# One V projection per quad, one PSUM bank for the output sums, 37 resident weight halves

## The chip, the cores and the metric

The kernel runs on one core of a Trainium2 chip. That core has five engines with queues of their own: TensorE (PE; its weight loads are shown apart, as PEld) multiplies, VectorE (DVE) and ScalarE (ACT) work on tiles in SBUF and read the PSUM accumulators, GpSimd (POOL) works on SBUF alone, and SyncE (SP) issues DMAs. The metric is the device time of one execution in microseconds (us): the median of the runs.

## The reference

An input of 2048 rows by 640 features goes through four layers, each added to its input after a layer norm: A, B, A, B.

Layer A is attention with a recurrent memory. The rows are cut into 64 segments of 32. To each segment the 8 rows of memory are put in front, so that 40 rows are worked on:

```python
for s in range(n_seg):
    h = jnp.concatenate([mem, xs], axis=1)
    q, k, v = (einsum('btd,dhe->bhte', h, W) for W in (Wq, Wk, Wv))
    p = softmax(mask(q @ k.T * scale))
    o = einsum('bhte,hed->btd', p @ v, Wo)
    mem = o[:, :M, :].copy()
    outs.append(o[:, M:, :])
```

There are 32 heads of 192. The memory of a segment is the first 8 rows of the output of the one before, so the segments follow one another.

Layer B is attention with 32 heads of 20 in which a row sees eight rows: itself and those 2, 4 and so on to 14 rows before it.

## The kernel before

**Lanes and steps.** The two A layers run side by side as two lanes. Lane 1 (the second A layer) is two segments (LAG = 2) behind lane 0. A step `t` works on segment t in lane 0 and segment t - 2 in lane 1; both use the same weights, so one matmul has 80 columns, 40 of each lane. There are 66 steps with layer A and one last step with B alone. In the first two and the last two of the 66 one lane is empty, and matmuls have 40 columns. Layer B of step t - 1 (called b) is done for both lanes inside step t.

**Quads.** The 32 heads are taken four at a time, in eight quads. For a quad, `a_k`, `a_q` and `a_v` call `proj` (30 matmuls into one bank, L247) and copy the result out of PSUM: K by ACT into KF and Kz (L259 to L261), Q by VectorE into QT (L266), V by VectorE into vT (L275). `a_vt` turns vT round with six transposes on TensorE (ps_vt, L282), and VectorE copies that to Vt (L284). `a_s` makes the scores from KF, Kz and QT with eight matmuls (ps_s, L294 and L295), takes their exponent on ACT (E, L297) and masks it on VectorE (Em, L300). `a_pv` multiplies Em and Vt (ps_o, L313; eight matmuls), and ACT works out the reciprocal of the softmax sums by four logarithms and an exponent (R, L317 and L319). `a_norm` scales ps_o by R into OT (VectorE, L328, L337, L338); it can be split so that the last two operations come later. `a_o` multiplies OT by the output weights, 30 matmuls that add up over all eight quads (ps_acc, L351), five quads (OLAG) later.

**PSUM.** There are eight banks. Four go by number: bank 0 holds ps_k, bank 1 ps_q and ps_s in turn, bank 2 ps_v and ps_vt, bank 3 what layer B and the layer norms write. Bank 0 takes V of quad 1, layer B's K (ps_bk) and every second of its scores (ps_bs) as well, bank 3 the transposes of quad 1. ps_o has two banks, and the output sums two: chunks 0 and 1 in one, 2 to 4 in the other. A tile is written only when all that read the one before it in its bank are done.

**Order.** The order of all five queues is written out by hand in `step`: each engine does its work in the order of the program. In quad i (0 to 6) this is K and Q of i, a part of layer B (`b_first`), PV of i - 1, V of i + 1, a second part of layer B (`b_second`), an output group, the norm of i - 1, layer B's masks (`b_mask`, L487), the scores of i, and the transposes of V of i + 1. V is so one quad ahead, and there are two each of vT and Vt. Quad 0 has V of 0, the statistics of layer B's layer norm (`b_ln`: ten matmuls into ps_st, L379, three small operations on VectorE, two on ACT, L394 and L396), V of 1, the transposes of 0, the scores, layer B's centring and scaling (`b_ln_apply`, L402 and L408) and the transposes of 1. Quad 7 has K, PV of 6, Q, two output groups round its scores, the statistics of the next step's layer norm (`ln1`), PV of 7 and the other output groups.

At the end of a step `mem_out` copies the memory rows of the output sums into the next step's input hT (VectorE, L367, one copy for each bank of the sums), and `b_x1` adds the rest to the residual (L418). The last output group therefore finishes chunk by chunk, and the K of quad 0 goes through its input chunk by chunk:

```python
order = [(m, c) for m in (0, 2) for c in range(NC)] + [(m, c) for c in range(NC) for m in (3, 5, 1, 4)]   # last output group
order = [(n, c) for c in range(NC) for n in range(6)]                                                      # K of quad 0
```

Layer B's scores (`b_s`, L478, L480) stand in quads 2 to 4, two of six in each (in ps_bs of bank 0 and bank 3). Their operand QX is made by POOL (L470), their PV (`b_pv`, L500) is in quads 4 and 5.

**Weights.** The weights of layer A are 64 halves of 128 x 1920 (480 KB). 36 stay in SBUF after the first step; the other 28 are streamed in every step through a ring of six, in an order that `half_order` and `resident_halves` spread evenly over TensorE's work. `prefetch` issues each half from SP as two DMAs of 960 columns (L211), as soon as a ring place comes free (`used`).

Of the kernel before, what the change touches and what calls it, by code (L numbers as in the profile page):

```python
# [42 lines left out]
N_RES = 36  # L43
# [5 lines left out]
def half_order():  # L49

    quad = 15 * (NT + MM)
    other = [2 * NX * NC, 2 * NBC * NC * NX, NC * NC * NX + 2 * BHC * NX, NC * P + 2 * BHC * NX, 11 * NX, 5 * NX,
             3 * P + NC * NC * NX, 2 * NX * NC]
    order = []
    for i in range(NQUAD):
        kinds = [("k", i), ("q", i)] + ([("v", 0)] if i == 0 else []) + ([("v", i + 1)] if i < NQUAD - 1 else [])
        for kind, j in kinds:
            order += [((kind, j, h), quad) for h in range(2)]
        last = order.pop()
        order.append((last[0], last[1] + 16 * (NT + MM) + other[i]))  # L60
# [18 lines left out]
class Kernel:  # L79
    def __init__(self, ctx, tc, A_x, A_mem0, A_Wq, A_Wk, A_Wv, A_Wo, B_wqkv, B_wo, out):  # L80
        self.tc = tc
        self.nc = tc.nc
        self.x = A_x
        self.mem0 = A_mem0
        self.out = out
        self.n_seg = A_x.shape[0]
        self.wsrc = {"k": A_Wk, "q": A_Wq, "v": A_Wv, "o": A_Wo}
        pool = lambda name, bufs, **kw: ctx.enter_context(tc.tile_pool(name=name, bufs=bufs, **kw))
        self.cp = pool("consts", 1)
        self.wres = pool("wres", 1)  # L90
# [12 lines left out]
        self.resident = resident_halves(order)  # L103
        self.loads = [u for u, _ in order] + [u for _ in range(self.n_seg + LAG - 1) for u, _ in order if u not in self.resident]
        self.ring_free = RING
        self.B_wqkv, self.B_wo = B_wqkv, B_wo
        self.build_consts()

    def build_consts(self):
# [90 lines left out]
    def prefetch(self):  # L200

        while self.loads and (self.loads[0] in self.resident or self.ring_free):
# [7 lines left out]
            for c0 in range(0, HALF, PIECE):  # L210
                self.nc.sync.dma_start(out=t_[:, c0:c0 + PIECE], in_=self.wsrc[kind][i, h, :, c0:c0 + PIECE])  # L211
# [22 lines left out]
    def acc_of(self, c):  # L234

        return self.acc[int(c >= 2)], c - 2 * int(c >= 2)

    def proj(self, kind, i, t):
# [3 lines left out]
        ps = self.big(f"ps_{kind}", 0 if kind == "v" and i == 1 else {"k": 0, "q": 1, "v": 2}[kind])  # L242
# [26 lines left out]
    def a_v(self, i, t):  # L269


        nc = self.nc
        ps = self.proj("v", i, t)
        vT = self.vT[i % 2]
        nc.vector.tensor_copy(out=self.cols(vT[:]), in_=self.cols(ps[:, 0:6 * NT].rearrange("p (a n) -> p a n", a=6)))  # L275

    def a_vt(self, i):

        nc = self.nc
        ps = self.ps_big.tile([P, 6, P], BF16, name="ps_vt", tag=f"bank{3 if i == 1 else 2}")  # L280
        for n in range(6):
            nc.tensor.transpose(out=ps[:, n, :], in_=self.vT[i % 2][:, n, :], identity=self.ident[:])  # L282
        vt = self.Vt[i % 2]
# [20 lines left out]
    def a_pv(self, i):  # L304
# [3 lines left out]
        em, vt = self.em, self.Vt[i % 2]  # L308
# [13 lines left out]
    def a_norm(self, i, split=False):  # L322
# [4 lines left out]
        self.norm = ov, r, oc  # L327
        nc.vector.tensor_tensor(out=oc[:, :, 0:3:2], in0=ov[:, :, 0:4:3], in1=r, op=ALU.mult)  # L328
        self.ots[i] = ot
        if not split:  # L330
            self.a_norm_mid()

    def a_norm_mid(self):

        nc = self.nc
        ov, r, oc = self.norm
        nc.vector.tensor_tensor(out=oc[0:64, :, 1], in0=ov[0:64, :, 1], in1=r[0:64, :, 0], op=ALU.mult)  # L337
        nc.vector.tensor_tensor(out=oc[64:P, :, 1], in0=ov[64:P, :, 2], in1=r[64:P, :, 1], op=ALU.mult)  # L338

    def a_o(self, i):  # L340
# [8 lines left out]
        for m, c in order:  # L349
            acc, k = self.acc_of(c)  # L350
            nc.tensor.matmul(self.cols(acc[:, k]), lhsT=w[m // 3][:, m % 3, P * c:P * (c + 1)], rhs=self.cols(ot[:, m]),  # L351
                             start=(i == 0 and m == 0 and k == 0), stop=(i == NQUAD - 1 and m == 4), skip_group_check=True)
# [6 lines left out]
    def mem_out(self, t):  # L359
# [5 lines left out]
        for acc, cs in zip(self.acc, (slice(0, 2), slice(2, NC))):  # L365
            a = acc[:].rearrange("p c (l n) -> p c l n", l=2)
            nc.vector.tensor_copy(out=h[:, cs, self.l0:self.l1, 0:NM], in_=a[:, :, self.l0:self.l1, 0:NM])  # L367
# [6 lines left out]
    def ln_stats(self, x, sq):  # L374
        nc = self.nc
        ps = self.big("ps_st", 3)
# [34 lines left out]
    def b_x1(self, b):  # L411
# [4 lines left out]
        for acc, cs in zip(self.acc, (slice(0, 2), slice(2, NC))):  # L416
            a = acc[:].rearrange("p c (l n) -> p l c n", l=2)
            nc.vector.tensor_tensor(out=x1[:, on, cs], in0=a[:, on, :, NM:LT], in1=xin[:, on, cs], op=ALU.add)  # L418
# [6 lines left out]
    def b_ln(self, b):  # L425
        self.bmr = self.ln_rstd(*self.ln_small(self.ln_stats(self.x1[b], self.bsq)))
# [15 lines left out]
    def b_k(self, b):  # L442
        ps = self.b_proj(D, "ps_bk", 0)
# [45 lines left out]
    def b_pv(self, g):  # L489
# [5 lines left out]
        ps = self.big("ps_bo", 3)  # L495
# [24 lines left out]
    def b_wo(self, b):  # L520
        nc = self.nc
        ps = self.big("ps_by", 3)
# [22 lines left out]
    def ln1(self, t):  # L545
        x = self.xin[t % 2]
        self.amv = self.ln_small(self.ln_stats(x, self.asq))
# [33 lines left out]
    def b_second(self, b, i):  # L581
# [4 lines left out]
        if 2 <= i <= 4:  # L586
            self.b_s(b, 2 * i - 4)
            self.b_s(b, 2 * i - 3)
# [4 lines left out]
    def step(self, t):  # L593
# [51 lines left out]
        self.a_pv(6)  # L645
# [3 lines left out]
        self.a_norm(6, split=True)  # L649
        self.a_o(7 - OLAG)  # L650
        self.a_s()
        self.a_norm_mid()
# [3 lines left out]
        self.a_pv(7)  # L656
# [89 lines left out]
```

## Time and profile before

| | |
|---|---|
| median of 3 runs | 3343.12 us (3337.2 to 3345.89) |
| the profiled execution | 3337.32 us, its span 3335.6 us |
| granted TensorE clock, mean | 0.983 |
| busy: PE, PEld, DVE, ACT, POOL | 3205.4, 3101.4, 2258.0, 1870.7, 308.6 us |
| read from HBM | 931.93 MB, 280 GB/s over the span |
| first K of the second step | about 101 us |
| one step in the middle, K of quad 0 to the next | 49.26 us (1838.24 to 1887.50) |

The span runs from the first to the last instruction on the core. A row of a timeline gives the start and the duration in us, the engine, the line, the operation, output and inputs and how many instructions are merged, and in brackets the idle time before it and what ended that. The end of a matmul is modelled and lies about 0.2 us behind its start, while the next one starts 0.036 us later; so the pace of TensorE is read from start to start. A row of the waits gives who waited for whom, the total in us, how often, and the longest.

### The profile page before, as it was taken

The numbers are of one execution on the slowest core, as the hardware profiler recorded it, in microseconds if no ns is written. First come the engines' busy times: TensorE is split into PE (matmuls) and PEld (weight loads), VectorE is DVE, ScalarE is ACT, GpSimd is POOL, SyncE is SP. The second block draws the span as 40 slices with busy tenths as digits, with TensorE's granted clock in tenths as the row PEclk, the third lists the DMA queues.
The fourth block names the chain that finished last, engine by engine and source line by source line (L and its number), as shares of the span: only waits on it lengthen the run. The fifth ranks groups of instructions, "written<-read, shape, count | busy, mean of one in ns | idle before, by whom it ended". The sixth has DMA issues, their size and how long they took to land.

```text
span 3335.6 us, 191059 instructions
## 1 busy us (share of the span) xinstructions
PE 3205.4 (96%) x85536; PEld 3101.4 (93%) x85536; DVE 2258.0 (68%) x5953; ACT 1870.7 (56%) x5743; POOL 308.6 (9%) x486
## 2 busy tenths in 40 slices
PE   5799999999999999999999999999999999999997
PEld 4799999999999999999999999999999999999996
DVE  2477677677677677677767767767767767766665
ACT  2365565555555556556556556555555655655654
POOL 1001001001001001101100100100100100110111
PEclk6799999999999999999999999999999999999999
DMA  9988888888888888888888888888888888888886
GB/s 348 305 285 283 280 286 282 281 285 283 281 285 280 282 293 282 284 287 284 283 279 287 281 278 285 283 281 286 283 279 289 286 280 289 278 288 286 279 287 216
DMA packets 555365, 947.01 MB, mean 284 GB/s; under 512 B 69936, under 2 KB 554288, under 8 KB 554416
## 3 DMA queue, kind: packets, MB, share of 16 engines
q1 hardware_dynamic: 542880, 926.32, 84.3%
q8 instruction: 669, 10.96, 1.3%
q10 hardware_dynamic: 11664, 8.48, 0.8%
q14 instruction: 152, 1.25, 0.1%
HBM read 931.93 MB, written 2.62 MB: 280 GB/s over the span
## 4 chain that ended last, share of the span: by engine, by line
PE 81%; DVE 7%; DMA 5%; ACT 4%; issue 2%; SPq 1%; DVEq 0%
PE ps_k L247 17%; PE ps_v L247 16%; PE ps_q L247 15%; PE ps_acc L351 13%; PE ps_vt L282 6%; DVE vT L275 4%; PE ps_o L313 4%; DMA w_ring<-in_A_Wk_dram 3%; ACT R L317 2%; PE ps_bk L438 2%; PE ps_bq L438 2%; PE ps_by L525 1%; PE ps_bv L438 1%; PE ps_s L294 1%; PE ps_s L295 1%
## 5 line engine op out<-in xcount | busy, mean ns | idle before, releaser
L247 PEld LDWEIGHTS <-w_ring 128*128 128x128 bf16 x20790 | 848.7, 100 | 45.4 <-issue 13.5
L317 ACT ACTIVATE R<-ps_o 64x160 f32<-64x160 f32 (+1 forms) x2112 | 620.2, 294 | 313.3 <-ACT Kz L261 142.8
L266 DVE CAST QT<-ps_q 128x480 bf16<-128x480 f32 (+1 forms) x528 | 339.4, 643 | 400.6 <-PE ps_q L247 400.3
L259 ACT CAST KF<-ps_k 128x320 bf16<-128x320 f32 (+1 forms) x528 | 220.7, 418 | 692.1 <-PE ps_k L247 692.1
L470 POOL TENSOR_TENSOR QX<-QB,hmask 128x384 bf16<-128x384 bf16 (+1 forms) x396 | 291.0, 756 | 2964.1 <-ACT QB L449 2473.7
L275 DVE CAST vT<-ps_v 128x480 bf16<-128x480 f32 (+1 forms) x528 | 339.4, 643 | 295.1 <-PE ps_v L247 279.7
L247 PE MATMUL ps_v<-hT,w_v 128*128 128x80 bf16 (+1 forms) x10890 | 475.6, 201 | 6.2 <-DMA w_v<-in_A_Wv_dram 3.2
L351 PE MATMUL ps_acc<-OT,w_o 128*128 128x80 bf16 (+1 forms) x8910 | 440.6, 201 | 14.0 <-DMA w_o<-in_A_Wo_dram 7.9
L247 PE MATMUL ps_k<-hT,w_ring 128*128 128x80 bf16 (+1 forms) x8910 | 421.1, 200 | 13.3 <-issue 5.0
L247 PEld LDWEIGHTS <-w_v 128*128 128x128 bf16 x10890 | 420.5, 100 | 8.0 <-DMA w_v<-in_A_Wv_dram 4.3
L247 PE MATMUL ps_q<-hT,w_q 128*128 128x80 bf16 (+1 forms) x8910 | 404.8, 201 | 4.8 <-DMA w_q<-in_A_Wq_dram 3.2
L351 PE MATMUL ps_acc<-OT,w_ring 128*128 128x80 bf16 (+1 forms) x6930 | 390.4, 201 | 5.4 <-DMA w_ring<-in_A_Wo_dram 3.7
L351 PEld LDWEIGHTS <-w_o 128*128 128x128 bf16 x8910 | 371.0, 100 | 17.6 <-DMA w_o<-in_A_Wo_dram 9.7
L328 DVE TENSOR_TENSOR OT<-ps_o,R 128x320 bf16<-128x320 f32 (+1 forms) x528 | 254.3, 482 | 164.4 <-ACT R L319 149.2
L247 PEld LDWEIGHTS <-w_q 128*128 128x128 bf16 x8910 | 349.9, 100 | 6.0 <-DMA w_q<-in_A_Wq_dram 5.1
L247 PE MATMUL ps_k<-hT,w_k 128*128 128x80 bf16 (+1 forms) x6930 | 340.9, 201 | 3.8 <-issue 3.0
L247 PE MATMUL ps_q<-hT,w_ring 128*128 128x80 bf16 (+1 forms) x6930 | 323.0, 201 | 7.6 <-DMA w_ring<-in_A_Wq_dram 6.8
L351 PEld LDWEIGHTS <-w_ring 128*128 128x128 bf16 x6930 | 310.1, 100 | 7.8 <-DMA w_ring<-in_A_Wo_dram 5.2
L282 PE MATMUL ps_vt<-ident,vT 128*128 128x128 bf16 x3168 | 269.5, 222 | 35.0 <-DVE vT L275 1.3
L284 DVE COPY Vt<-ps_vt 80x768 bf16<-80x768 bf16 x528 | 290.8, 551 | 10.8 <-PE ps_vt L282 0.5
L247 PEld LDWEIGHTS <-w_k 128*128 128x128 bf16 x6930 | 290.2, 100 | 4.7 <-issue 3.7
L297 ACT ACTIVATE E<-ps_s 80x320 bf16<-80x320 f32 (+1 forms) x528 | 223.5, 423 | 99.0 <-PE ps_s L295 92.6
(94 smaller groups left out, 4619.7 us busy)
## 6 DMA issues: line engine op xcount, KB each, us to landing
w_ring<-in_A_Wk_dram SPq DMA_DIRECT2D x1188, 240.0 KB, 4.2
w_ring<-in_A_Wq_dram SPq DMA_DIRECT2D x924, 240.0 KB, 4.5
w_ring<-in_A_Wo_dram SPq DMA_DIRECT2D x924, 240.0 KB, 4.5
w_ring<-in_A_Wv_dram SPq DMA_DIRECT2D x660, 240.0 KB, 4.4
w_v<-in_A_Wv_dram SPq DMA_DIRECT2D x22, 240.0 KB, 5.2
w_q<-in_A_Wq_dram SPq DMA_DIRECT2D x18, 240.0 KB, 5.0
w_o<-in_A_Wo_dram SPq DMA_DIRECT2D x18, 240.0 KB, 5.0
w_k<-in_A_Wk_dram SPq DMA_DIRECT2D x14, 240.0 KB, 5.0
```

Of the source, the lines that this page charges most:

```text
L247: nc.tensor.matmul(ps[:, NT * n + self.c0:NT * n + self.c1], lhsT=w[n // 3][:, c, P * (n % 3):P * (n % 3 + 1)], rhs=hT[:, NT * c + self.c0 ...
L259: nc.scalar.copy(out=kf, in_=pv[:, :, 0:3:2, :])
L266: self.nc.vector.tensor_copy(out=self.cols(qt[:]), in_=self.cols(ps[:, 0:6 * NT].rearrange("p (a n) -> p a n", a=6)))
L275: nc.vector.tensor_copy(out=self.cols(vT[:]), in_=self.cols(ps[:, 0:6 * NT].rearrange("p (a n) -> p a n", a=6)))
L282: nc.tensor.transpose(out=ps[:, n, :], in_=self.vT[i % 2][:, n, :], identity=self.ident[:])
L284: nc.vector.tensor_copy(out=vt[0:NT, 0:4 * VH].rearrange("p (a x) -> p a x", a=2)[:, :, 0:512].rearrange("p a (b c) -> p a b c", b=2)[:, : ...
L297: nc.scalar.activation(out=self.cols(e[0:NT]), in_=self.cols(sv[0:NT]), func=ACT.Exp, scale=float(DH) ** -0.5)
L317: nc.scalar.activation(out=self.cols(r[r0:r0 + 64, :, j]), in_=self.cols(src), func=ACT.Ln)
L328: nc.vector.tensor_tensor(out=oc[:, :, 0:3:2], in0=ov[:, :, 0:4:3], in1=r, op=ALU.mult)
L351: nc.tensor.matmul(self.cols(acc[:, k]), lhsT=w[m // 3][:, m % 3, P * c:P * (c + 1)], rhs=self.cols(ot[:, m]), start=(i == 0 and m == 0 an ...
L438: nc.tensor.matmul(ps[:, NX * n:NX * (n + 1)], lhsT=self.wqkv[:, c, e0:e0 + P], rhs=self.h2T[:, c, :], start=(c == 0), stop=(c == NC - 1))
L470: self.nc.gpsimd.tensor_tensor(out=qx[:, 0:nh, :], in0=self.qb[:, c, :].unsqueeze(1).to_broadcast([P, nh, NX]), in1=self.hmask[:, 0:nh].un ...
```

## The change

- V of a quad is made in its own quad, after PV of the quad before. The transposes of V of quad i come behind K of quad i + 1 (in quad 7 there are two: those of 6 behind K, those of 7 behind the scores). One vT and one Vt are left.
- The output sums are one tile in one bank. The bank that is free by this is bank 4, used by layer B alone: statistics, K, every second score, the second PV, the output. Layer B has banks 3 and 4, layer A 0 to 2. The two copies of the memory rows stay, of the same tile.
- Of layer B's two scores in a quad the second comes behind layer A's scores. The masks of both move to the next quad, ahead of the Q copy.
- The norm of quad 6 is no longer split.
- 37 halves stay in SBUF, 27 are streamed. The order of loads follows the new order of V.
- The first load of each of the 64 halves is one DMA of 1920 columns; later ones are two of 960 as before.

```diff
-N_RES = 36
+N_RES = 37
...
-        self.Vt = pers("Vt", [P, 4 * VH], 2, zero=False)
-        for v in self.Vt:
-            nc.vector.memset(v[:], 1.0)
-        self.vT = pers("vT", [P, 6, P], 2)
+        self.Vt = pers("Vt", [P, 4 * VH], 1, zero=False)[0]
+        nc.vector.memset(self.Vt[:], 1.0)
+        self.vT = pers("vT", [P, 6, P], 1)[0]
...
-            for c0 in range(0, HALF, PIECE):
-                self.nc.sync.dma_start(out=t_[:, c0:c0 + PIECE], in_=self.wsrc[kind][i, h, :, c0:c0 + PIECE])
+            piece = HALF if self.n_loaded < N_HALVES else PIECE
+            self.n_loaded += 1
+            for c0 in range(0, HALF, piece):
+                self.nc.sync.dma_start(out=t_[:, c0:c0 + piece], in_=self.wsrc[kind][i, h, :, c0:c0 + piece])
...
-        ps = self.big(f"ps_{kind}", 0 if kind == "v" and i == 1 else {"k": 0, "q": 1, "v": 2}[kind])
+        ps = self.big(f"ps_{kind}", {"k": 0, "q": 1, "v": 2}[kind])
...
-            self.acc = [self.ps_one.tile([P, n, NT], F32, name=f"ps_acc{n}", tag=f"acc{n}") for n in (2, 3)]
+            self.acc = self.ps_one.tile([P, NC, NT], F32, name="ps_acc", tag="acc")
...
-        for acc, cs in zip(self.acc, (slice(0, 2), slice(2, NC))):
-            a = acc[:].rearrange("p c (l n) -> p c l n", l=2)
-            nc.vector.tensor_copy(out=h[:, cs, self.l0:self.l1, 0:NM], in_=a[:, :, self.l0:self.l1, 0:NM])
+        a = self.acc[:].rearrange("p c (l n) -> p c l n", l=2)
+        for cs in (slice(0, 2), slice(2, NC)):
+            nc.vector.tensor_copy(out=h[:, cs, self.l0:self.l1, 0:NM], in_=a[:, cs, self.l0:self.l1, 0:NM])
...
-        ps = self.b_proj(D, "ps_bk", 0)
+        ps = self.b_proj(D, "ps_bk", 4)
...
-        ps = self.big("ps_bs", 3 * (c % 2))
+        ps = self.big("ps_bs", 4 - c % 2)
...
-        ps = self.big("ps_bo", 3)
+        ps = self.big("ps_bo", 3 + g)
...
         for i in range(NQUAD - 1):
             if a:
                 self.a_k(i, t)
+                if i >= 1:
+                    self.a_vt()
+            if b is not None and 3 <= i <= 5:
+                self.b_mask(b, 2 * i - 6)
+                self.b_mask(b, 2 * i - 5)
+            if a:
                 self.a_q(i, t)
             if b is not None:
                 self.b_first(b, i)
             if a and i >= 1:
-                self.a_pv(i - 1)
+                self.a_pv()
             if a:
-                self.a_v(0 if i == 0 else i + 1, t)
-            if i == 0:
-                if b is not None:
-                    self.b_ln(b)
-                if a:
-                    self.a_v(1, t)
-                    self.a_vt(0)
+                self.a_v(i, t)
+            if b is not None and i == 0:
+                self.b_ln(b)
             if b is not None:
                 self.b_second(b, i)
             if a and i >= OLAG:
                 self.a_o(i - OLAG)
             if a and i >= 1:
                 self.a_norm(i - 1)
-            if b is not None and 2 <= i <= 4:
-                self.b_mask(b, 2 * i - 4)
-                self.b_mask(b, 2 * i - 3)
             if a:
                 self.a_s()
             if b is not None and i == 0:
                 self.b_ln_apply(b)
+            if b is not None and 2 <= i <= 4:
+                self.b_s(b, 2 * i - 3)
             if b is not None and i == 6:
                 self.b_wo(b)
-            if a:
-                self.a_vt(i + 1)
...
         self.a_k(7, t)
-        self.a_pv(6)
+        self.a_vt()
         self.a_q(7, t)
         if nt < T:
             self.ln1_sq(nt)
-        self.a_norm(6, split=True)
+        self.a_pv()
+        self.a_v(7, t)
         self.a_o(7 - OLAG)
+        self.a_norm(6)
         self.a_s()
-        self.a_norm_mid()
+        self.a_vt()
         self.a_o(8 - OLAG)
```

More of the change, by code (lines that the diff above doesn't have):

```diff
@@ L55, in half_order @@
     for i in range(NQUAD):
-        kinds = [("k", i), ("q", i)] + ([("v", 0)] if i == 0 else []) + ([("v", i + 1)] if i < NQUAD - 1 else [])
-        for kind, j in kinds:
-            order += [((kind, j, h), quad) for h in range(2)]
+        for kind in "kqv":
+            order += [((kind, i, h), quad) for h in range(2)]
         last = order.pop()
-        order.append((last[0], last[1] + 16 * (NT + MM) + other[i]))
+        order.append((last[0], last[1] + 16 * (NT + MM) + 6 * (P + MM) + other[i]))
         for j in ([i - OLAG] if i < NQUAD - 1 else range(i - OLAG, NQUAD)):
@@ L273, in a_v, with a_vt @@
         ps = self.proj("v", i, t)
-        vT = self.vT[i % 2]
-        nc.vector.tensor_copy(out=self.cols(vT[:]), in_=self.cols(ps[:, 0:6 * NT].rearrange("p (a n) -> p a n", a=6)))
-    def a_vt(self, i):
+        nc.vector.tensor_copy(out=self.cols(self.vT[:]), in_=self.cols(ps[:, 0:6 * NT].rearrange("p (a n) -> p a n", a=6)))
+    def a_vt(self):
         nc = self.nc
-        ps = self.ps_big.tile([P, 6, P], BF16, name="ps_vt", tag=f"bank{3 if i == 1 else 2}")
+        ps = self.ps_big.tile([P, 6, P], BF16, name="ps_vt", tag="bank2")
         for n in range(6):
-            nc.tensor.transpose(out=ps[:, n, :], in_=self.vT[i % 2][:, n, :], identity=self.ident[:])
-        vt = self.Vt[i % 2]
+            nc.tensor.transpose(out=ps[:, n, :], in_=self.vT[:, n, :], identity=self.ident[:])
+        vt = self.Vt
         nc.vector.tensor_copy(out=vt[0:NT, 0:4 * VH].rearrange("p (a x) -> p a x", a=2)[:, :, 0:512].rearrange("p a (b c) -> p a b c", b=2)[:, :, :, 0:DH],
@@ L320, in a_pv, with a_norm @@
         self.ov, self.r = ov, r
-    def a_norm(self, i, split=False):
+    def a_norm(self, i):
         nc = self.nc
@@ L326, in a_norm @@
         oc = self.cols(ot[:])
[L327 removed]
         nc.vector.tensor_tensor(out=oc[:, :, 0:3:2], in0=ov[:, :, 0:4:3], in1=r, op=ALU.mult)
[L329 to L336 removed]
         nc.vector.tensor_tensor(out=oc[0:64, :, 1], in0=ov[0:64, :, 1], in1=r[0:64, :, 0], op=ALU.mult)
         nc.vector.tensor_tensor(out=oc[64:P, :, 1], in0=ov[64:P, :, 2], in1=r[64:P, :, 1], op=ALU.mult)
+        self.ots[i] = ot
     def a_o(self, i):
@@ L415, in b_x1 @@
         on = slice(self.l0, self.l1)
-        for acc, cs in zip(self.acc, (slice(0, 2), slice(2, NC))):
-            a = acc[:].rearrange("p c (l n) -> p l c n", l=2)
-            nc.vector.tensor_tensor(out=x1[:, on, cs], in0=a[:, on, :, NM:LT], in1=xin[:, on, cs], op=ALU.add)
+        a = self.acc[:].rearrange("p c (l n) -> p l c n", l=2)
+        for cs in (slice(0, 2), slice(2, NC)):
+            nc.vector.tensor_tensor(out=x1[:, on, cs], in0=a[:, on, cs, NM:LT], in1=xin[:, on, cs], op=ALU.add)
         for l in range(2):
```

28 lines of the change are left out of this document (12 added, 16 removed).

## The prediction

> **What bounds the kernel now.** I read the page first. In its slices TensorE is busy nine tenths and more from the fourth slice to the last but one, and the DMA engines eight tenths:
>
> ```profile
> span 3335.6 us, 191059 instructions
> PE   5799999999999999999999999999999999999997
> ...
> DMA  9988888888888888888888888888888888888886
> ```
>
> So all but the start and the end is a TensorE stream, and the question is which of its waits goes and which comes. In the waits of the stretch 203.8 to 3171 us no row names a DMA; the largest of TensorE's own is this:
>
> ```profile
> PEld L282 <- DVE vT L275: 64.0, 237, 0.4
> ```
>
> The transposes wait for VectorE's copy of V, 237 times in 60 steps. The idle time is short of the loss, since a weight load counts as busy for 100 ns, so I went to the timeline of one step, between two starts of K of quad 0: 1838.24 and 1887.50, that is 49.26 us. TensorE in its quads 0 and 2:
>
> ```profile
> 1843.43 0.20 PE L295 MATMUL ps_s<-QT,Kz 128*128 128x80 bf16 x1
> 1843.76 0.51 PE L282 MATMUL ps_vt<-ident,vT 128*128 128x128 bf16 x6
> ...
> 1854.91 0.20 PE L295 MATMUL ps_s<-QT,Kz 128*128 128x80 bf16 x1
> 1855.26 0.51 PE L282 MATMUL ps_vt<-ident,vT 128*128 128x128 bf16 x6
> 1855.79 1.24 PE L247 MATMUL ps_k<-hT,w_ring 128*128 128x80 bf16 x30
> ```
>
> Read starts, not ends: 30 matmuls take 1.07 us from start to start of the next group (0.036 each), eight of scores 0.29, six transposes 0.34, ten of layer norm 0.30. From 1843.43 to 1843.76 are 0.33 where 0.04 are due: 0.29 lost. The VectorE and then the ACT rows beside it:
>
> ```profile
> 1844.20 0.32 DVE L300 TENSOR_TENSOR Em<-E,maskA 80x320 bf16<-80x320 bf16 x1
> 1844.45 0.48 DVE L402 TENSOR_TENSOR ln_xc<-x,ln_m 128x320 f32<-128x320 bf16 x1
> 1844.96 0.56 DVE L408 TENSOR_TENSOR h2T<-ln_xc,ln_r 128x160 bf16<-128x160 f32 x2
> 1845.44 0.55 DVE L284 COPY Vt<-ps_vt 80x768 bf16<-80x768 bf16 x1
> ```
>
> ```profile
> 1843.08 0.35 ACT L394 ACTIVATE ln_v<-ln_v,eps_t 128x64 f32<-128x64 f32 x1 [2.64 <-DVE ln_v L389]
> 1843.46 0.26 ACT L396 ACTIVATE ln_r<-ln_v 128x64 f32<-128x64 f32 x1
> 1843.74 0.43 ACT L297 ACTIVATE E<-ps_s 80x320 bf16<-80x320 f32 x1
> ```
>
> The reader is to see one chain: layer norm's small operations (VectorE, 1842.25 to 1842.98, behind vT of quad 0), ACT's two of them, then E, Em, the centring and scaling, and only then Vt. Now it lies beside V of quad 1 (1.07) and its transposes (0.34). That is what the change moves away.
>
> **What goes, per step.** (a) The wait of transposes for vT: 0.29 in quad 0, 0.31, 0.30 and 0.30 in quads 2 to 4: 1.20. vT is ready 0.92 after V ends (0.20 to the copy's start, 0.66, 0.06); behind the next K at least 1.36 lie between (scores 0.29, K 1.07), so it goes whole. (b) K behind transposes: 1855.26 to 1855.79 is 0.53 where 0.34 is due; with 0.11, 0.07 and 0.07 at the others 0.44. These K wait for bank 0, where layer B's scores and K are still read; with a bank for B it goes. (c) 0.24 before the last PV (1882.64 due, 1882.88 seen), which waited for the split second half of a norm; the halves are joined earlier. (d) About 0.10 inside layer B's score pair. Sum 1.98.
>
> **What comes.** (e) Quad 0. V starts at 1840.40 and layer norm's ten matmuls at 1841.47, as now. V of 1 and its transposes are out, so scores start at 1841.77, K of 1 at 1842.06, transposes at 1843.13, Q of 1 would at 1843.47. Q shares bank 1 with the scores; E ends at 1844.17 in its place behind layer norm's two, plus 0.06: 1844.23, a wait of 0.76. Q ends at 1845.30. PV needs Vt, now made in the slot of the row at 1845.44, because Em, centring and scaling stand ahead in VectorE's order: done 1845.99, plus 0.07. PV at 1846.06, another 0.76. Together 1.52; on TensorE all of V, Q and K queue behind. Bounds 1.3 (E 0.1 and Vt 0.1 sooner) and 1.7.
>
> (f) K of quad 0. Memory rows of the sums are copied into hT before K can begin. Today the first copy starts at 1887.26, while the second bank is still written, and K follows O without a gap:
>
> ```profile
> 1887.26 0.19 DVE L367 CAST hT<-ps_acc 128x32 bf16<-128x32 f32 x1 [0.42 <-PE ps_acc L351]
> ...
> 1887.45 0.20 PE L351 MATMUL ps_acc<-OT,w_o 128*128 128x80 bf16 x1
> 1887.50 0.27 PE L247 MATMUL ps_k<-hT,w_ring 128*128 128x80 bf16 x3
> ...
> 1887.68 0.21 DVE L367 CAST hT<-ps_acc 128x48 bf16<-128x48 f32 x1 [0.24 <-PE ps_acc L351]
> ```
>
> With one bank the first copy starts where the second does, 1887.68; plus 0.19 and 0.07, K at 1887.94 instead of 1887.50: 0.44. Whether a reader of some columns waits for a whole bank, one place shows: in the prologue ln_m reads only the first five matmuls' columns, written by 12.66, and starts at 12.96, just after the second five end at 12.93. Bounds 0 (by columns) and 0.5; I take 0.44.
>
> (g) Layer B's masks, moved between Vt and QT. After V of quad 4 ends (0): bs and scores 0.46, bs 0.06, K 1.07, transposes 0.34, Q 1.07: layer B's PV at 3.00. VectorE: norm waits for R to 0.94 (PV ended at -1.07, four Ln 1.23 and an Exp 0.47 from 0.22 later); norms to 2.00, Em to 2.35, Vt to 2.93, two masks (0.36 and 0.22, starts overlapping by 0.08) to 3.35, plus 0.06: a wait of 0.4 in quad 5. In quad 4 one mask suffices and a longer bs precedes: 3.27 against 3.10, 0.1 to 0.2. I take 0.50 for both; bounds 0.2 and 0.8 (a masks' row each way). QT is late with it, but scores come 1.5 us after.
>
> Costed at nothing: one vT and one Vt (each was last read half a quad or more before it is written again); E ahead of the odd EB on ACT (KF starts 0.2 late, under 2.5 us of cover); POOL's QX, 0.8 each, wanted 4.5 us after their release; V and transposes of 7 in the tail, where Vt is done 1.66 after the scores and PV due at 1.71: a thin cover of 0.05, which costs 0.1 when gone (in the bounds of g). A 37th resident half cuts transfers by 1 in 28 and SP's issues from 56 to 54; as no DMA is waited for, nothing. The "issue" rows of that stretch, some 21 us, may shrink with less traffic: bounds 0 and -21, taken 0.
>
> (h) First loads whole: the first step, to 101 us, waits for weights. At 50 to 70 us they come at 366 to 373 GB/s in 1,920-byte rows; at 70 to 80 us, with layer B's 19,200-byte rows among them, 408. 31.5 MB at 370 are 85 us, at 408 are 77: -8 to +0.5 (TensorE starts on a half only when it is whole). 3,840 bytes lie between; I take -4.
>
> The Trainium skill, page "DMA: Bandwidth & Descriptors", section Bandwidth, gives 0.95 us for 64 KB and 6.15 for 1 MB; an estimate by a straight line between is 3.8 us for two of 240 KB and 3.2 for one of 480, 16% less, which would make (h) -14 and the sum 3360. The trace, with transfers queued, has a half every 1.25 us, so I hold to the rates above.
>
> **Sum.** 1.52 + 0.44 + 0.50 - 1.98 = +0.48 per step. 62 steps have both lanes and three more layer B and one lane, which I price alike: 65 x 0.48 = 31, less 4: +27. The profiled execution took 3337.3, 5.8 below the median; on it 3364, on the median 3343.1 + 27 = 3370. Own range: +0.30 to +0.70 a step, 3358 to 3385.
>
> **Rivals.** *Columns*: the copies wait for their own columns alone. (f) goes: +0.04 a step, 65 x 0.04 - 4 = -1: 3342, not slower. It decides once K of quad 0 follows O within 0.1 us. For it: two copies are kept. Against: the row at 12.96. 8 in 100.
>
> The Trainium skill, page "PSUM — Partial Sum Buffer", section Terms, calls a read by one engine during a write by another in the same bank and quadrant an error; by that rule this rival could not be, and 3370 stands.
>
> *The layer norm chain is short*: if E and Vt came before layer norm's operations, (e) would vanish: -1.04 a step, 3343 - 68 - 4 = 3271. The orders on ACT and VectorE are written out, and E stands behind ln_r in the rows above though its scores ended earlier. 7 in 100.
>
> *VectorE fills up*: in quads 3 to 5 its operations (Vt 0.55, masks 0.72, QT 0.66, B's 0.9, vT 0.66, norms 1.13, Em 0.32: 4.9) exceed TensorE's 4.7. If the lag carries into PV and scores, 0.1 a quad and one more miss in the tail add 0.4: +0.88, 3396. Against: quad 5 has 1.07 of O to catch up. 12 in 100.
>
> *DMA matters after all*: the 21 us of "issue" go too: 3370 - 21 = 3349, no change by the bound below. For it: each step has a loss of some 0.3 us that comes and goes. Against: those rows name no DMA. 4 in 100.
>
> **Numbers.** The forecast has 69 in 100. About 0.3%, 10 us, can be told from no change here, which is 3333 to 3353. Faster: the short chain's 0.07 and, as *columns* spreads over some 10 us each way, 0.02 of its 0.08. Same: the other 0.06 and the 0.04 of the DMA rival. Slower: 0.69 and 0.12. The range 3342 to 3393 holds the forecast, the DMA rival, the upper half of *columns* and nearly half of the full VectorE: 0.69 + 0.04 + 0.04 + 0.05 = 0.82.
>
> **What would show it.** Right: no wait of L282 for vT; Q of quad 1 behind E, PV of 0 behind Vt, 0.7 to 0.8 each; K of quad 0 0.4 after O; layer B's second PV behind a mask; steps of 49.7. Wrong: steps under 49.3, K of quad 0 on O's heels, or Q of 1 straight behind the transposes.

## The result, and the profile after

| | median us | lowest to highest | runs |
|---|---|---|---|
| before, same chip | 3340.17 | 3334.25 to 3345.89 | 11 |
| after | 3332.22 | 3326.05 to 3338.79 | 11 |

The ratio is 0.9974, with a 95% interval of 0.9964 to 0.9985: the changed kernel is 0.26% faster, 8 us, a little under what I had called tellable. The forecast was +27 us, so it missed by 35 us. The profiled execution took 3332.15 us. Further below, the profiled execution of the kernel with 33 halves took 13,100.66 us, about four times its other three; it is left out, and what slowed it stays open. From the page of after, the span, the slices of TensorE and of DMA, and two queues (packets, MB, share):

```profile
span 3330.3 us, 191039 instructions
PE   5899999999999999999999999999999999999997
DMA  9888888888888888888888888888888888888886
q1 hardware_dynamic: 514944, 894.35, 82.8%
q8 instruction: 668, 10.94, 1.3%
```

The second slice of TensorE has gone from 7 to 8 and that of DMA from 9 to 8; the rest looks as before. The waits of 203.8 to 3171 us (engine, line and tile that waits, what released it, us in total, times, longest), with other engines left out:

```profile
PEld L244 <- issue: 67.0, 125, 1.0
...
PEld L309 <- DVE Vt L280: 42.2, 59, 0.7
...
PE ps_o L309 <- DVE Vt L280: 34.4, 59, 0.6
PE ps_q L244 <- ACT E L293: 23.9, 40, 0.9
...
PE ps_k L244 <- DVE hT L354: 7.3, 26, 0.3
```

The wait of transposes for vT, the largest of before, has no row any more. In its place PV waits for Vt once per step (59 times), Q for E, and K of quad 0 for the copy of the sums. The "issue" row is the weight loads of that same Q and K, which stand still while their matmuls wait: in the step below 0.71 and 0.38 us, and 60 times both is 65 of the 67.0. TensorE in the step from 2029.08 to 2078.49 us (start, busy time, line, operation), around quad 0:

```profile
2027.80 0.99 PE L338 MATMUL ps_acc<-OT,w_o 128*128 128x80 bf16 x23
...
2029.08 0.27 PE L244 MATMUL ps_k<-hT,w_ring 128*128 128x80 bf16 x3 [0.28 <-DMA w_ring<-in_A_Wv_dram]
...
2032.87 0.70 PE L244 MATMUL ps_k<-hT,w_ring 128*128 128x80 bf16 x15
...
2033.95 0.50 PE L278 MATMUL ps_vt<-ident,vT 128*128 128x128 bf16 x6
2035.04 0.70 PE L244 MATMUL ps_q<-hT,w_ring 128*128 128x80 bf16 x15 [0.59 <-ACT E L293]
2035.57 0.70 PE L244 MATMUL ps_q<-hT,w_q 128*128 128x80 bf16 x15
2036.86 0.46 PE L309 MATMUL ps_o<-Em,Vt 80*128 80x80 bf16 x8 [0.58 <-DVE Vt L280]
```

Six transposes need 0.34, so Q of quad 1 was due at 2034.29 and starts at 2035.04: 0.75 late. PV was due at 2036.11 and starts at 2036.86: 0.75 late again. K of quad 0 starts 0.45 late, behind the copies of the sums (line 354); the profile puts this wait down to the copy in 26 of the 60 steps and to a DMA in 34, and a run below tells which it is. VectorE and then ACT beside it:

```profile
2028.83 0.30 DVE L354 CAST hT<-ps_acc 128x32 bf16<-128x32 f32 x2 [0.84 <-PE ps_acc L338]
...
2035.27 0.48 DVE L389 TENSOR_TENSOR ln_xc<-x,ln_m 128x320 f32<-128x320 bf16 x1
2035.78 0.56 DVE L395 TENSOR_TENSOR h2T<-ln_xc,ln_r 128x160 bf16<-128x160 f32 x2
2036.26 0.55 DVE L280 COPY Vt<-ps_vt 80x768 bf16<-80x768 bf16 x1
```

```profile
2033.90 0.35 ACT L381 ACTIVATE ln_v<-ln_v,eps_t 128x64 f32<-128x64 f32 x1 [2.64 <-DVE ln_v L376]
2034.28 0.26 ACT L383 ACTIVATE ln_r<-ln_v 128x64 f32<-128x64 f32 x1
2034.56 0.43 ACT L293 ACTIVATE E<-ps_s 80x320 bf16<-80x320 f32 x1
```

E still stands behind layer norm's two operations and Vt behind its centring and scaling, as in the trace of before; only now TensorE waits for both.

Where the time went, from the starts of K of quad 0 in both traces. "Commonest" is the length that occurs most often among the 62 two-lane steps; "irregular" is their mean less that.

| | start to the third step | commonest step | irregular per step |
|---|---|---|---|
| before | 154.5 | 49.26 | 0.25 |
| after | 141.4 | 49.42 | 0.22 |

Between these two executions the two-lane steps lose 8 us (62 x 0.16, less 2 of irregular loss), the start gains 13. So nothing of this gain lies in the steps that most of the change is about.

### The profile page after: what moved, and what is told of

It reads as the page before. It is cut to its first block, busy times and chain, and to the rows that moved or that the text cites. A ratio compares the mean times of both kernels' runs of the same rounds, so it can differ in the third digit from the quotient of the medians.

```text
span 3330.3 us, 191039 instructions
## 1 busy us (share of the span) xinstructions
PE 3157.9 (95%) x85536; PEld 3092.7 (93%) x85536; DVE 2235.0 (67%) x5951; ACT 1850.8 (56%) x5743; POOL 308.6 (9%) x486
## 3 DMA queue, kind: packets, MB, share of 16 engines
q1 hardware_dynamic: 514944, 894.35, 82.8%
## 4 chain that ended last, share of the span: by engine, by line
PE 84%; DVE 6%; DMA 5%; ACT 2%; issue 2%; SPq 0%; ACTq 0%; DVEq 0%
PE ps_v L244 17%; PE ps_k L244 15%; PE ps_q L244 14%; PE ps_acc L338 14%; PE ps_o L309 5%; PE ps_vt L278 5%; DMA w_ring<-in_A_Wv_dram 3%; PE ps_s L290 2%; PE ps_s L291 2%; PE ps_bq L425 2%; PE ps_bk L425 2%; PE ps_bs L465 2%; PE ps_by L512 1%; PE ps_bv L425 1%; PE ps_bo L487 1%
## 5 line engine op out<-in xcount | busy, mean ns | idle before, releaser
L244 PEld LDWEIGHTS <-w_ring 128*128 128x128 bf16 x19800 | 813.3, 100 | 98.1 <-issue 77.6
L244 PE MATMUL ps_q<-hT,w_q 128*128 128x80 bf16 (+1 forms) x11880 | 508.1, 201 | 5.4 <-issue 3.4
L244 PE MATMUL ps_k<-hT,w_ring 128*128 128x80 bf16 (+1 forms) x9900 | 466.6, 201 | 27.4 <-DMA w_ring<-in_A_Wv_dram 9.8
L244 PEld LDWEIGHTS <-w_q 128*128 128x128 bf16 x11880 | 460.6, 100 | 7.1 <-issue 3.7
L244 PE MATMUL ps_v<-hT,w_v 128*128 128x80 bf16 (+1 forms) x9900 | 438.6, 201 | 6.3 <-DMA w_v<-in_A_Wv_dram 5.9
L244 PEld LDWEIGHTS <-w_v 128*128 128x128 bf16 x9900 | 384.4, 100 | 7.7 <-DMA w_v<-in_A_Wv_dram 6.9
L244 PE MATMUL ps_k<-hT,w_k 128*128 128x80 bf16 (+1 forms) x5940 | 304.9, 201 | 3.6 <-issue 2.2
L296 DVE TENSOR_TENSOR Em<-E,maskA 80x320 bf16<-80x320 bf16 (+1 forms) x528 | 190.2, 360 | 164.6 <-ACT E L293 151.4
L338 PEld LDWEIGHTS <-w_ring 128*128 128x128 bf16 x6930 | 292.0, 100 | 9.0 <-DMA w_ring<-in_A_Wo_dram 4.7
L244 PE MATMUL ps_v<-hT,w_ring 128*128 128x80 bf16 (+1 forms) x5940 | 276.1, 201 | 6.3 <-DMA w_ring<-in_A_Wv_dram 6.3
L309 PE MATMUL ps_o<-Em,Vt 80*128 80x80 bf16 (+1 forms) x4224 | 236.9, 199 | 40.0 <-DVE Vt L280 38.9
```

Source lines behind the costliest of these rows:

```text
L244: nc.tensor.matmul(ps[:, NT * n + self.c0:NT * n + self.c1], lhsT=w[n // 3][:, c, P * (n % 3):P * (n % 3 + 1)], rhs=hT[:, NT * c + self.c0 ...
L296: nc.vector.tensor_tensor(out=self.cols(em[0:NT]), in0=self.cols(e[0:NT]), in1=self.cols(self.maskA[0:NT, :]).unsqueeze(1).to_broadcast([N ...
L309: nc.tensor.matmul(self.cols(ov[:, pr, k]), lhsT=vt[0:NT, 2 * VH * pr + c0:2 * VH * pr + c0 + P], rhs=self.cols(em[0:NT, 2 * pr + k // 2]) ...
L338: nc.tensor.matmul(self.cols(self.acc[:, c]), lhsT=w[m // 3][:, m % 3, P * c:P * (c + 1)], rhs=self.cols(ot[:, m]), start=(i == 0 and m == ...
```

## The experiments

My theory after this result: the first loads are worth more than I gave them (h); the steps' terms are right but for the masks (g); and the 37th half does something after all, within the irregular loss. The rivals were that the start's gain comes from the new order rather than from the loads, that the terms offset each other in other sizes, and that the irregular loss has another cause than the traffic. The first four runs shared a chip, on which the kernel before took 3352.25.

**First loads alone, and the change without them.** The kernel before with

```diff
-            for c0 in range(0, HALF, PIECE):
+            piece = HALF if self.n_loaded < N_HALVES else PIECE
+            self.n_loaded += 1
+            for c0 in range(0, HALF, piece):
```

and the kernel after with

```diff
-            piece = HALF if self.n_loaded < N_HALVES else PIECE
+            piece = PIECE
```

> The kernel before, with the first load of each half as one DMA and nothing else changed. The start is measured by the start of K of quad 0 in the third step: 154.5 us before, 141.4 us in the changed kernel. Theory 'rows' (the longer rows of the first loads are what shortened the start): the first step falls from 86.4 to about 79 us, the third step's K starts at 142 to 147, the steps stay at 49.26, the total falls by 8 to 12 us (0.24 to 0.36%). Rival 'the rest' (shorter memsets ahead of the first x load, the order of the loads, the 37th half): the first step falls by at most 4 us, the third step's K starts at 150 or later, total 0 to -4 us.

> The changed kernel, with the first loads in two pieces as before. Theory 'rows': the first step is back at 86 us, the third step's K starts at 150 to 155, the steps stay at 49.41, the total is 3341 to 3345, slower than the kernel before by 0 to 0.2%. Rival 'the rest': the third step's K starts at 145 or earlier and the total stays at 3332 to 3336.

| | third step starts | commonest | ratio | 95% |
|---|---|---|---|---|
| before, whole first loads | 139.6 | 49.27 | 0.9974 | 0.9963 to 0.9984 |
| after, loads in pieces | 151.8 | 49.43 | 0.9998 | 0.9986 to 1.0009 |

The loads alone give the whole of the 0.26%, and without them the rest of the change comes to nothing. The busy time of each engine, granted clock, DMA share and GB/s, in stretches of ten us, before and then after, tell why:

```profile
20.00:30.00 10.00, 7.25 (x194) 6.17 (x190) 3.86 (x11) 3.43 (x15) 1.00 (x5) 0.85 0.98 341
30.00:40.00 10.00, 6.38 (x118) 5.09 (x119) 2.22 (x7) 2.34 (x10) 0.00 (x0) 0.50 0.97 324
...
50.00:60.00 10.00, 7.17 (x137) 5.66 (x134) 3.25 (x11) 2.19 (x9) 0.00 (x0) 0.50 1.03 373
```

```profile
20.00:30.00 10.00, 6.88 (x159) 5.94 (x160) 3.48 (x12) 2.49 (x10) 1.08 (x6) 0.55 1.02 389
30.00:40.00 10.00, 7.03 (x153) 5.97 (x150) 2.77 (x8) 2.81 (x12) 0.00 (x0) 0.50 1.03 406
...
50.00:60.00 10.00, 6.54 (x143) 5.54 (x142) 2.55 (x9) 2.19 (x9) 0.00 (x0) 0.50 1.03 403
```

Both keep the DMA engines full, but between 20 and 60 us the whole halves come at 389 to 406 GB/s where the pieces came at 324 to 379; in the kernel before with whole first loads alone it is 402 to 404. I had taken my rate for before from 50 to 70 us alone; from 20 to 40 us it was slower, 341 and 324.

**Layer norm's operations moved behind E and Vt.** The kernel after, with ln_r asked for after the scores of quad 0 and the centring and scaling after the transposes of quad 0:

```diff
     def b_ln(self, b):
-        self.bmr = self.ln_rstd(*self.ln_small(self.ln_stats(self.x1[b], self.bsq, 4)))
+        self.bmv = self.ln_small(self.ln_stats(self.x1[b], self.bsq, 4))
...
                 if i >= 1:
                     self.a_vt()
+            if b is not None and i == 1:
+                self.b_ln_apply(b)
...
             if b is not None and i == 0:
-                self.b_ln_apply(b)
+                self.bmr = self.ln_rstd(*self.bmv)
```

> The changed kernel, with layer B's two ACT operations of the layer norm behind the scores' exponent, and its centring and scaling behind the first Vt copy (still ahead of the Q copy of quad 1). Theory (the two waits of 0.74 and 0.75 in quad 0 are layer norm's chain and nothing else): both go, the step falls from 49.41 to 47.9, the total by 1.5 x 63 = 94 us to about 3238 (ratio 0.969). Rival 'VectorE fills up': the operations that are moved make the Q copy, V's copy or h2T late, at most half of it is gained: 48.7 or more, 3285 or more.

Ratio 0.974 (0.972 to 0.976), 3264.56 us; the commonest step is 47.92, that is 1.50 less than 49.42, where (e) had 1.52. TensorE in quads 0 and 1 of such a step:

```profile
1893.51 0.70 PE L244 MATMUL ps_k<-hT,w_k 128*128 128x80 bf16 x15
1894.05 0.50 PE L278 MATMUL ps_vt<-ident,vT 128*128 128x128 bf16 x6
1894.38 0.70 PE L244 MATMUL ps_q<-hT,w_ring 128*128 128x80 bf16 x15
1894.92 0.70 PE L244 MATMUL ps_q<-hT,w_q 128*128 128x80 bf16 x15
1895.46 0.45 PE L309 MATMUL ps_o<-Em,Vt 80*128 80x80 bf16 x8
1895.74 0.70 PE L244 MATMUL ps_v<-hT,w_v 128*128 128x80 bf16 x15
```

Every start follows the one before at the bare price, and no row ends in a wait. (e) is settled, mechanism and size, and nothing of it comes back elsewhere in the commonest step: VectorE, which a rival had filling up, did not take the 1.50 away. The total I had at 0.969; what it lacks lies in the irregular loss, 0.56 per step in this trace.

**The sums' banks.** The kernel before with the sums in one tile, as the change has them; and that with layer B's K and even scores in bank 4, out of K's bank:

```diff
-            self.acc = [self.ps_one.tile([P, n, NT], F32, name=f"ps_acc{n}", tag=f"acc{n}") for n in (2, 3)]
+            self.acc = self.ps_one.tile([P, NC, NT], F32, name="ps_acc", tag="acc")
...
-        ps = self.b_proj(D, "ps_bk", 0)
+        ps = self.b_proj(D, "ps_bk", 4)
...
-        ps = self.big("ps_bs", 3 * (c % 2))
+        ps = self.big("ps_bs", 4 - c % 2)
```

> The kernel before, with the output sums as one tile in one bank and nothing else changed. Theory (a copy waits for the whole bank): K of quad 0 starts 0.45 us after the last output matmul's turn, the commonest step rises from 49.26 to 49.70. Rival 'columns': it stays at 49.26.

> The same, and the bank that is free by it is given to layer B's K and every second score, in the order of before. Theory (the 0.11, 0.19, 0.07 and 0.07 us of K behind the transposes are waits for bank 0): the commonest step falls from 49.70 to 49.27 again, the late starts of K behind the transposes go to 0.02 or less. Rival: they are what a matmul costs behind transposes that had to wait, and stay.

The first took 3375.26 in its one execution, where the kernel before ranged from 3343.64 to 3360.35; its commonest step is 49.68, which is +0.42. The second took 3343.44 with 49.26: the commonest step is back, and the trace has no late K behind transposes any more. So one bank is what holds K of quad 0, (f) costs 0.42 to 0.45, (b) gives 0.43, and they cancel, as forecast. In the trace of after, K of quad 0 is 0.447 late in the median step.

**Layer B's PV behind that of layer A in quads 4 and 5**, on top of the kernel with the late layer norm:

```diff
-            if b is not None:
+            if b is not None and not 4 <= i <= 5:
                 self.b_first(b, i)
             if a and i >= 1:
                 self.a_pv()
+            if b is not None and 4 <= i <= 5:
+                self.b_first(b, i)
```

> The changed kernel with layer B's layer norm chain behind the scores and the first Vt copy, and with layer B's PV of quads 4 and 5 behind layer A's PV. Theory: the second edit takes the 0.11 us waits of both of layer B's PV (0.22 a step) away, as the masks are done by then; commonest step 47.92 - 0.22 = 47.70; total 0.970 of the kernel before, less whatever the weights' traffic takes back at this pace. Rival: layer B's VectorE operations come later by this and delay V's copy, so that a wait of the same size comes up at the transposes: 47.9.

Ratio 0.9716 (0.9701 to 0.973), commonest step 47.65: 0.27 less, where 0.22 was expected. In the trace of after the starts show what was there to win, 0.25 in quad 5 and 0.02 in quad 4; TensorE and VectorE of quad 5:

```profile
2056.74 0.70 PE L244 MATMUL ps_q<-hT,w_ring 128*128 128x80 bf16 x15
2057.28 0.59 PE L487 MATMUL ps_bo<-VB,EB 128*128 128x41 bf16 x7
2057.71 0.45 PE L309 MATMUL ps_o<-Em,Vt 80*128 80x80 bf16 x8
```

```profile
2056.66 0.55 DVE L280 COPY Vt<-ps_vt 80x768 bf16<-80x768 bf16 x1
2057.13 0.48 DVE L474 TENSOR_TENSOR EB<-EB,mB 128x384 bf16<-128x384 bf16 x2
```

The masks end about where I had them (3.32 us after V of quad 4, forecast 3.35). But layer B's PV is a row of matmuls over three EB tiles, and TensorE runs those of the first tiles before the last mask is done. Only the last part waits.

**How many halves stay.** The kernel after with `N_RES` at 36 and, on another chip beside the kernel after once more, at 35 and 33:

```diff
-N_RES = 37
+N_RES = 35
```

> The changed kernel with 36 resident halves as before, so 28 streamed in a step. Theory: no step waits for weights, the commonest step stays at 49.41, the total within 0.1% of 3332. Rival 'traffic': the irregular loss per step (mean less commonest step: 0.25 before, 0.19 after) comes from the weights' traffic; it goes back to 0.25, and the total rises by 4 us or more, more than that if waits for w_ring come up.

> The changed kernel itself, as the measure for the two beside it on the same chip. Commonest step 49.41 to 49.43, total 0.9974 of the kernel before (0.996 to 0.999).

> The changed kernel with 35 resident halves: 29 streamed in a step instead of 27. Theory 'traffic' (what the 37th half gave, some 10 us, is a shorter irregular loss, which grows with the weights' traffic): the commonest step stays at 49.42, the mean step lies further above it than with 37 (by 0.3 us more), the total is 15 to 30 us above the changed kernel on the same chip. Rival 'no waits, no price' (the forecast's zero; 36 halves were slower by chance of the set or of the chip): total within 5 us of the changed kernel.

> The changed kernel with 33 resident halves: 31 streamed. Theory 'traffic': the irregular loss goes on growing, total 35 to 80 us above the changed kernel, and waits that name w_ring come up. Rival: within 10 us.

| halves kept | streamed per step | median us | ratio | 95% | commonest | irregular |
|---|---|---|---|---|---|---|
| 37 (first result) | 27 | 3332.22 | 0.9974 | 0.9964 to 0.9985 | 49.42 | 0.22 |
| 37 (again) | 27 | 3339.39 | 0.9975 | 0.9964 to 0.9985 | 49.42 | 0.26 |
| 36 | 28 | 3356.59 | 1.0008 | 0.9992 to 1.0025 | 49.43 | 0.59 |
| 35 | 29 | 3372.21 | 1.0076 | 1.0046 to 1.0106 | 49.42 | 0.91 |
| 33 (three executions) | 31 | 3400.47 | 1.0156 | 1.0132 to 1.018 | – | – |

I had expected no wait from the 36th to the 37th; there is one, about 0.34% or 11 us (2 to 20 by the two intervals), and 33 and 61 us for two and four halves. In the traces of 35 to 37 halves the commonest step does not move by more than 0.01: all of it is in the irregular loss. `N_RES` also changes which halves are streamed; no run changes their number alone.

What that loss is, the order of instructions tells. I numbered all instructions of TensorE's queue in the trace (weight loads, matmuls and 138 to 399 that handle semaphores) from the start of the program and looked at every wait inside a group of matmuls, between 204 and 3100 us, that no regular cause explains. In the kernel before, all 44 fall at number 193 or 194 of 256; so do all 26 in after, all 79 with layer B's PV moved, and all 108 with 35 halves. In 97 of 100 of these waits TensorE goes on 1.2 to 1.6 us after a packet of 16,384 bytes of the instruction queue (q8) has ended; of random moments, 8% lie so. The trace of after has 85,536 weight loads, 85,536 matmuls and 141 other instructions of TensorE's queue, 171,213 in all; divided by 256 that is 668.8, and the page counts 668 such packets. The kernel before has 261 instructions more, 669.8 blocks of 256, and 669 packets.

So TensorE here waits for its own instructions, which come by DMA in blocks of 256. Counted over the 62 two-lane steps, with waits between groups, what TensorE loses at this place is the irregular loss within 0.1 us per step in every trace but that of the thirds below: 0.28 in before, 0.20 and 0.29 in the two of after, 0.61 with 36 halves, 0.99 with 35. That the blocks come late because weights are ahead of them on the DMA engines is inferred from what lengthens the waits (above, and below); no trace shows which engine a packet waits on.

**Longer and shorter rows in every step.** With every half as one DMA of 3,840-byte rows, once in the kernel with both moves and once in after (`piece = HALF`); with thirds of 1,280 bytes (`PIECE = 640`) in after:

> The changed kernel with both edits to the order, and every weight half, not only the first loads, as one DMA of 3,840-byte rows. Theory 'traffic': the same bytes keep the DMA engines busy some 4% less (a row of 3,840 bytes took 152 ns, two of 1,920 take 158, and half the closing writes go), so the irregular loss of some 0.6 us a step falls; the total is 0 to 15 us below the kernel with both edits, ratio to the kernel before 0.967 to 0.972. Rival 'coarser loads are late': a half is usable only when all of it has landed and is waited for, commonest step above 47.7 or waits for w_ring up, total 5 us or more above.

> The changed kernel with every weight half as one DMA. Theory 'traffic': commonest step 49.42, the irregular loss of 0.2 to 0.3 a step falls by a part, total 0 to 10 us below the changed kernel, ratio to the kernel before 0.994 to 0.9975. Rival 'coarser loads are late': above 0.9985.

> The changed kernel, with the streamed halves in three DMAs of 640 columns (1,280-byte rows) instead of two of 960. All irregular waits lie at one place in every 256 instructions of TensorE's stream and end 1.3 to 1.5 us after a 16 KB packet of the instruction queue, so they are waits for instructions. Theory 'rows' (such a packet waits behind the weights' rows that are ahead on its DMA engine, the longer the rows the longer): the irregular loss falls from 0.26 us a step to 0.05 to 0.2, the total by 3 to 12 us below the changed kernel, ratio to the kernel before 0.994 to 0.997. Rival 'busy share' (what counts is how busy the DMA engines are; shorter rows and more closing writes make them busier): it rises to 0.4 or more, ratio 1.000 or more.

| | bytes a row | ratio | 95% | commonest | irregular | us per step at the place of 256 |
|---|---|---|---|---|---|---|
| after in thirds | 1,280 | 1.0046 | 1.0031 to 1.006 | 49.42 | 0.67 | 0.08 |
| after (again) | 1,920 | 0.9975 | 0.9964 to 0.9985 | 49.42 | 0.26 | 0.29 |
| after whole | 3,840 | 1.0163 | 1.0137 to 1.019 | 49.43 | 1.36 | 1.40 |
| both moves | 1,920 | 0.9716 | 0.9701 to 0.973 | 47.65 | 0.66 | 0.67 |
| both moves, whole | 3,840 | 0.9989 | 0.9968 to 1.001 | 47.65 | 2.24 | 2.15 |

The last two columns are of one trace each; the three traces with the order of after, 27 streamed halves and rows of 1,920 bytes (after twice, and that with its first loads in pieces) span 0.20 to 0.36 at that place. The same bytes stream in all five. The whole rows keep the weights' queue busy for less of the span (packets, MB, share):

```profile
q1 hardware_dynamic: 262224, 894.24, 80.4%
```

against 82.8% in after; and yet TensorE stands five times as long at that place (124 of 124 such waits, and 182 of 182 with both moves). So it is not the share of busy time that counts, as the theory behind these two runs had it. What does change is when the packets of instructions begin: each takes 0.96 to 1.00 us in the median, whatever the rows, but it begins later after TensorE has passed the last such place: 1.19 us with thirds, 1.47 in after (again), 1.80 in after with whole rows, and 1.74 and then 2.05 with both moves (medians, 204 to 3100 us). One of the waits, in the kernel after with whole rows:

```profile
2443.97 0.34 PE L244 MATMUL ps_q<-hT,w_q 128*128 128x80 bf16 x5
2447.25 1.06 PE L244 MATMUL ps_q<-hT,w_q 128*128 128x80 bf16 x25 [2.94 <-issue]
```

Q stops after five of its thirty matmuls, in a resident half, so no weight is missing; a 16,384-byte packet of instructions runs from 2444.81 to 2445.79, and Q goes on 1.46 us later. Thirds shorten these waits, as rows of a third would, but the total is worse, and for another reason. The waits of that kernel, 204 to 3150 us:

```profile
PEld L338 <- DMA w_ring<-in_A_Wo_dram: 11.6, 20, 1.7
...
PE ps_q L244 <- DMA w_ring<-in_A_Wk_dram: 11.0, 18, 0.9
...
PE ps_acc L338 <- DMA w_ring<-in_A_Wo_dram: 8.6, 14, 1.6
```

Here the weights themselves come late, at 85.0% of busy time of their queue: of the irregular 0.67 us per step only 0.08 lie at the place of 256, and most of the rest at output groups, K and Q, whose waits name w_ring. So 1,920 bytes stand between two losses.

**More halves kept, a shorter ring.** The kernel with both moves, and space taken from the ring of streamed halves:

```diff
-N_RES = 37
-RING = 6
+N_RES = 39
+RING = 4
```

and likewise 38 and 5.

> The kernel with both edits to the order, with a ring of five instead of six halves and the place given to a 38th resident half: 26 streamed. Theory: fewer bytes and fewer weights queued ahead of the instructions, irregular loss below the 0.66 us of that kernel, 0.2 to 0.5; commonest step 47.65; ratio 0.961 to 0.969. Rival: five places are too few, waits for w_ring take it back: 0.972 or more.

> The same with a ring of four and 39 resident: 25 streamed. Theory as above: irregular loss 0.1 to 0.4, ratio 0.957 to 0.967, as long as four places carry the load. Rival: waits for w_ring come up in every step (a half takes 4 to 5 us to land), commonest step above 48, ratio 0.975 or more.

| kept, ring | streamed per step | median us | ratio | 95% | irregular |
|---|---|---|---|---|---|
| 37, 6 (both moves) | 27 | 3253.38 | 0.9716 | 0.9701 to 0.973 | 0.66 |
| 38, 5 | 26 | 3243.89 | 0.9679 | 0.9663 to 0.9695 | 0.67 |
| 39, 4 | 25 | 3228.07 | 0.9634 | 0.9614 to 0.9654 | 0.36 |

```profile
span 3226.4 us, 190662 instructions
...
PE 3124.9 (97%) x85536; PEld 3079.4 (95%) x85536; DVE 2239.2 (69%) x5951; ACT 1852.5 (57%) x5743; POOL 309.1 (10%) x486
...
q1 hardware_dynamic: 477504, 830.44, 80.6%
```

With 39 and 4, waits for weights cost 0.06 us per step, and what TensorE loses at the place of 256 falls from 0.67 to 0.30. At 3228.07 this is the fastest of all kernels run, 3.7% under the kernel before and 3.4% under the change. The middle one came out where I had it in total, but its irregular loss did not fall in the trace; one trace holds some dozens of these waits, and its mean is no finer than that.

## Why the prediction was wrong

By its own steps, us per step, gains negative:

| step | forecast | measured | from |
|---|---|---|---|
| (a) to (d) | -1.98 | -2.01 | starts, before against after; (b) also by two runs |
| (e) | +1.52 | +1.48; 1.50 | the same; late layer norm |
| (f) | +0.44 | +0.42; 0.42 | the same; one bank in before |
| (g) | +0.50 | +0.26; 0.27 | the same; PV moved |
| sum | +0.48 | +0.15; 0.16 | these four; commonest step |
| 37th half, whole run | 0 | about -11 (2 to 20) | 36 halves against 37 |
| (h), whole run | -4 | about -10 (5 to 12) | first loads alone |

- **(a), (b), (c), (d) and (e) were right.** The chain named in the first part, layer norm's small operations, ln_r, E, Em, the scaling, Vt, is what TensorE meets, and its price was right to 0.04. The rival that it is short fell with the same rows.
- **(f) was right**, and the rival of the columns fell: one tile alone makes the step 0.42 longer. The Trainium skill, page "PSUM — Partial Sum Buffer", section Terms, calls a read beside a write in one bank and quadrant an error; the trace agrees as far as it can, since K waits in every step. Whether the copies could read beside the writes wasn't tried.
- **(g) was mis-sized**, 0.26 for 0.50. The end of the masks was right; wrong was to let the whole of layer B's PV wait for the last of them. It reads three EB tiles one after another. With these 0.24, 0.04 of (e), 0.02 of (f) and 0.03 more that went, the sum per step was 0.32 too high (the four are rounded): 65 x 0.32 = 21 us of the 35.
- **The 37th half at nothing was wrong**, 11 us. The price stood in the text as a bound (the "issue" rows, 0 to -21) and as the rival that DMA matters after all, with 4 in 100. I dropped it because those rows name no DMA. A wait for instructions names nothing, though the instructions come by DMA.
- **(h) was mis-sized**, -10 (5 to 12) for -4, near its lower bound of -8 or beyond it. The rates from 50 to 70 us were taken for the whole first step, where 20 to 40 us ran at 341 and 324. The estimate from the Trainium skill, page "DMA: Bandwidth & Descriptors", section Bandwidth, of -14 was nearer in size. It reasons from DMAs that run one at a time, though, while here the queue was full: a row of 3,840 bytes took 153 ns and one of 1,920 took 79 in the median, nearly the same by the byte. The means between 20 and 70 us are 155 and 86: by these, whole halves need 10% less for the same bytes, and the first step fell from 86.4 us to 79.5 in after and 76.2 with the loads alone, 8 and 12%.
- **VectorE filling up** did not come: with the late layer norm the step falls by the whole 1.50.

Put together: +10 for the steps, -11 for the half, -10 for the loads is -11, against -8 measured. The two largest terms of the change, 2.01 gone and 2.16 come per step, nearly cancel, so the sign hung on three small ones, and each of the three erred the same way.

## What to carry to other kernels

When a wait is moved, follow the new chain for each consumer instruction and each tile that it reads, and don't let a group of matmuls wait as one block. Idle time that names no releaser is not free of the DMA: look for it at a fixed place in an engine's instruction stream, and price traffic by it. And before reordering a tuned loop, look for the operations that are queued ahead of the chain without being wanted yet: moving layer norm's few operations behind E and Vt was worth 2.3% of the changed kernel here, more than everything in the change.

## What was not expected of the hardware

- TensorE waits for its own instructions at one place of every 256, mostly 1.2 to 1.6 us after the end of a 16,384-byte packet of the instruction queue. With rows of 1,920 bytes that costs 0.20 to 0.36 us per step at 27 streamed halves (three traces in the order of after), 0.28 to 0.61 at 28 (five traces) and 0.99 at 29; where the step itself is shorter, as with both moves, it is 0.67 at 27. The traces are from several chips, so differences of about 0.1 mean little.
- The length of a row counts beyond the bytes. At the same traffic, rows of 1,280, 1,920 and 3,840 bytes cost 0.08, 0.29 and 1.40 us per step at that place; in the first step, where TensorE waits for weights, rows of 3,840 bytes are better than those of 1,920, 389 to 406 GB/s against 324 to 379 between 20 and 60 us.
- The kernel before had medians from 3340 to 3355 us in the five groups of runs, more than the whole effect of the change, so every ratio here is within one group.
